# One load queue, halved K and V loads and a shared wq/wo buffer in a decode attention and FFN kernel

## Chip, cores, metric

The kernel runs on one core of one Trainium2 chip. The metric is device time in microseconds (us), median over executions. The span of a profile is about 2 us shorter than the time of the same execution. GB/s are bytes that the core's 16 DMA engines moved, over time. In the profiles PE is the matrix engine (PEld its loads of weights), DVE the vector engine, ACT the scalar engine and SP the engine that here only issues loads; SBUF and PSUM are the core's own memories.

## The reference

```python
# x: 4 x 1 x 512; 32 query heads, 8 K/V heads, head size 128; the last 4096 of 16384 cached positions
xn = layernorm(x)
q  = xn @ wq                                   # wq 512 x 4096
o  = softmax(q k^T / sqrt(128)) v              # per batch and head, window of 4096
A  = o @ wo                                    # wo 4096 x 512
B  = (silu(xn @ w_gate) * (xn @ w_up)) @ w_down  # F = 1792
out = x + A + B
```

There is one query position, so nearly everything is reading: 32 groups (4 batches by 8 K/V heads) of 1 MiB of K and 1 MiB of V each, 67.1 MB, and 13.9 MB of weights.

## The kernel before

Weights come first. The K buffers are allocated after the buffer of wq is released, and lie where it lay. K tiles are loaded from the SP queue, V tiles from the ACT queue, each tile in one transfer with 8 KiB a partition. For each group PE transposes K (stage_T), multiplies it by q (stage_QK), ACT takes the exp, and PE multiplies by V (stage_PV). After each fourth group four heads of the output projection run.

```python
wq_pool = tc.alloc_tile_pool(name="wq_pool", bufs=1)
wq_sb = wq_pool.tile([P, KT, HD], bf16, name="wq_sb")
nc.sync.dma_start(out=wq_sb[:, :, :], in_=A_wq.rearrange("(k p) n -> p k n", p=P))
# ... layer norm, FFN (PSUM pool of 2 buffers), query projection ...
wq_pool.release()
k_pool = ctx.enter_context(tc.tile_pool(name="k_pool", bufs=5))
# ...
def stage_load(b, hk):
    k_nat = k_pool.tile([P, NCH, Dh], bf16, tag="knat")
    v_t = v_pool.tile([P, NCH, Dh], bf16, tag="v")
    nc.sync.dma_start(out=k_nat[:, :, :],
        in_=A_k_cache[b, hk, W0:W0 + W, :].rearrange("(p c) d -> p c d", c=NCH))
    nc.scalar.dma_start(out=v_t[:, :, :],
        in_=A_v_cache[b, hk, W0:W0 + W, :].rearrange("(p c) d -> p c d", c=NCH))
# ...
for gi in range(NG):
    if gi_load < NG:
        load_q.append(stage_load(*groups[gi_load]))   # two groups ahead
        # ...
    if pv_q:   stage_PV(pv_q.popleft())
    if qk_q:   pv_q.append(stage_QK(qk_q.popleft()))
    if load_q: qk_q.append(stage_T(load_q.popleft()))
```

The framework that builds the program orders the instructions of each engine by priority and readiness, so the order on an engine isn't always the order of the source.

The softmax here doesn't subtract the row's maximum and nothing guards it: scores larger than these inputs give would overflow.

## Time and profile before

| | before |
|---|---|
| time, median | 219.15 us (6 runs, 216.78 to 220.46) |
| profiled span | 216.2 us, granted clock 0.871 |
| bytes moved | 81.47 MB |
| DMA engines busy | nearly all of 2 to 203 us |
| PE busy | 72% of the span |

A DMA share of 1.00 in a window means that all 16 engines had work; the GB/s beside it tell how fast that work went. Both are needed below: the share can stay at 1 while the rate changes. The windows below count a packet's bytes where it starts. A transfer has *landed* when its semaphore is set, which in these traces comes some 0.4 us after its last packet has ended; ends of the stream are compared by that. Here are the page's rows of DMA issues (bytes each, then the median time from issue to landing) before.

```profile
v_t<-in_A_v_cache_dram ACTq DMA_DIRECT2D x32, 1024.0 KB, 13.2
k_nat<-in_A_k_cache_dram SPq DMA_DIRECT2D x32, 1024.0 KB, 12.5
```

The last V load alone is issued at 190.5 us, and the same view of the issues between 189 and 200 us gives its landing:

```profile
v_t<-in_A_v_cache_dram ACTq DMA_DIRECT2D x1, 1024.0 KB, 13.6
```

So it lands at 204.1 us (204.05 before rounding), and 12.1 us of the span follow. The prediction below takes 203.2 us and 13.0 us, from the window in which the last packets start; the load is still ending in the first 0.9 us of that tail.

### The profile page before, as it was taken

The page shows a single profiled execution, that of the slowest core. Times are in us where ns is not written, and L with a number is a line of the kernel's source. Part 1 is how long each engine was busy: PE and PEld are TensorE (multiplying, and loading weights), DVE is VectorE, ACT ScalarE, POOL GpSimd, SP SyncE. Part 2 cuts the span into 40 slices and gives each one's busy share as a digit, 9 for nine tenths or more (in the row PEclk, how much of TensorE's full clock was granted, in tenths as well). Part 3 has the DMA queues.
Part 4 walks back from the last instruction along what each step waited for, and adds up shares of the span by engine and source line. Part 5 has one row for each costly group of instructions (what it writes and reads, how often), then busy time and mean ns, then how long its engine had stood idle before and what let it go on. Part 6 is the DMA issues. An engine that isn't in the chain of part 4 may idle for free.

```text
span 216.2 us, 7353 instructions
## 1 busy us (share of the span) xinstructions
PE 156.2 (72%) x3394; PEld 135.4 (63%) x3394; DVE 112.1 (52%) x300; ACT 14.7 (7%) x39; POOL 0.7 (0%) x6
## 2 busy tenths in 40 slices
PE   0000368830698799987969997899799969969983
PEld 0000254320697697985968797689769947966980
DVE  4000353130376565865747684458657754854771
ACT  2000502000001000000100000000001000000010
POOL 1000000000000000000000000000000000000000
PEclk9999999965589959999997998579969997995895
DMA  6999999999999999999999999999999999999300
GB/s 216 418 417 398 356 368 406 406 372 389 415 426 415 411 418 415 400 424 415 414 417 417 414 415 418 412 418 417 412 420 418 414 420 415 412 421 381 127 3 1
DMA packets 16765, 81.47 MB, mean 377 GB/s; under 512 B 1112, under 2 KB 7008, under 8 KB 8032
## 3 DMA queue, kind: packets, MB, share of 16 engines
q1 hardware_dynamic: 9784, 43.78, 50.7%
q10 hardware_dynamic: 6952, 37.23, 42.5%
q8 instruction: 26, 0.43, 0.8%
q14 instruction: 3, 0.02, 0.0%
HBM read 81.01 MB, written 0.00 MB: 375 GB/s over the span
## 4 chain that ended last, share of the span: by engine, by line
PE 67%; issue 16%; DVE 9%; DMA 5%; ACTq 1%; ACT 1%
PE tp L208 31%; PE oT_ps L232 12%; PE st_ps L217 11%; PE out_acc L182 6%; DMA k_nat<-in_A_k_cache_dram 5%; PE out_acc L145 3%; PE q_ps L155 2%; PE a_ps L126 2%; DVE qT_all L162 1%; DVE aT L130 1%; ACT L86 1%; PE den_ps L248 0%; ACTq L195 0%; DVE kt_4253 L209 0%; DVE kt_3657 L209 0%
## 5 line engine op out<-in xcount | busy, mean ns | idle before, releaser
L208 PE MATMUL tp<-ident,k_nat 128*128 128x128 bf16 x1024 | 88.5, 236 | 17.6 <-DMA k_nat<-in_A_k_cache_dram 9.9
L208 PEld LDWEIGHTS <-k_nat 128*128 128x128 bf16 x1024 | 67.3, 105 | 23.4 <-issue 23.2
L232 PE MATMUL oT_ps<-p_sb,v_t 128*128 128x4 bf16 x1024 | 33.6, 165 | 3.0 <-issue 2.6
L232 PEld LDWEIGHTS <-v_t 128*128 128x128 bf16 x1024 | 32.2, 98 | 5.0 <-issue 4.8
L225 ACT ACTIVATE p_sb<-st_ps 128x128 bf16<-128x128 f32 x32 | 8.9, 277 | 167.3 <-PE st_ps L217 158.9
L111 PE MATMUL tp<-ident,xn_bf 4*128 4x4 bf16 x4 | 0.4, 165 | 24.5 <-DVE xn_bf L103 24.3
L111 PEld LDWEIGHTS <-xn_bf 4*128 4x128 bf16 x4 | 0.3, 102 | 24.5 <-DVE xn_bf L103 24.3
L182 PE MATMUL out_acc<-wo_sb,oT_all 128*4 128x512 bf16 x32 | 13.0, 552 | 0.5 <-DVE oT_all L251 0.5
L101 DVE RECIPROCAL rstd<-std 4x1 f32<-4x1 f32 x1 | 0.2, 151 | 18.3 <-ACT std L99 18.3
L162 DVE CAST qT_all<-q_ps 128x4 bf16<-128x4 f32 x32 | 4.6, 174 | 9.4 <-PE q_ps L155 9.1
L250 DVE RECIPROCAL rec<-den_ps 128x4 f32<-128x4 f32 x32 | 5.6, 176 | 6.5 <-PE den_ps L248 6.1
L209 DVE COPY kt_553<-tp 128x1024 bf16<-128x1024 bf16 x4 | 2.8, 691 | 11.3 <-PE tp L208 11.3
L241 DVE TENSOR_REDUCE dsum<-p_sb 128x4 bf16<-128x128 bf16 x32 | 8.2, 276 | 0.5 <-ACT p_sb L225 0.5
L155 PE MATMUL q_ps<-xnT,wq_sb 128*128 128x4 bf16 x128 | 5.7, 165 | 2.7 <-DVE qT_all L162 2.4
L155 PEld LDWEIGHTS <-wq_sb 128*128 128x128 bf16 x128 | 4.7, 101 | 4.3 <-issue 4.3
L248 PE MATMUL den_ps<-dsum,ones 128*128 128x4 bf16 x32 | 5.4, 169 | 1.8 <-issue 1.8
L182 PEld LDWEIGHTS <-oT_all 128*4 128x4 bf16 x32 | 2.6, 99 | 5.7 <-issue 4.3
L145 PE MATMUL out_acc<-wd_sb,hT 128*4 128x512 bf16 x14 | 5.8, 604 | 0.0
L251 DVE TENSOR_TENSOR oT_all<-oT_ps,rec 128x4 bf16<-128x4 f32 x32 | 5.2, 163 | 0.6
L126 PEld LDWEIGHTS <-wg_sb 128*128 128x128 bf16 x56 | 3.7, 105 | 3.0 <-issue 2.9
L209 DVE COPY kt_3537<-tp 128x1024 bf16<-128x1024 bf16 x4 | 2.7, 688 | 4.6 <-PE tp L208 4.6
L126 PE MATMUL a_ps<-xnT,wg_sb 128*128 128x4 bf16 x56 | 3.5, 166 | 2.1 <-DVE xnT L112 0.3
(125 smaller groups left out, 182.7 us busy)
## 6 DMA issues: line engine op xcount, KB each, us to landing
v_t<-in_A_v_cache_dram ACTq DMA_DIRECT2D x32, 1024.0 KB, 13.2
k_nat<-in_A_k_cache_dram SPq DMA_DIRECT2D x32, 1024.0 KB, 12.5
wq_sb<-in_A_wq_dram SPq DMA_DIRECT2D x1, 4096.0 KB, 15.8
wo_sb<-in_A_wo_dram SPq DMA_DIRECT2D x1, 4096.0 KB, 51.7
wg_sb<-in_B_w_gate_dram SPq DMA_DIRECT2D x1, 1792.0 KB, 22.2
wu_sb<-in_B_w_up_dram ACTq DMA_DIRECT2D x1, 1792.0 KB, 17.8
wd_sb<-in_B_w_down_dram ACTq DMA_DIRECT2D x1, 1792.0 KB, 30.0
x_sb<-in_A_x_dram ACTq DMA_DIRECT2D x1, 4.0 KB
```

The source lines that it names most:

```text
L126: nc.tensor.matmul(a_ps[:, :], wg_sb[:, kt, ft * P:(ft + 1) * P], xnT[:, kt, :], start=(kt == 0), stop=(kt == KT - 1),)
L145: nc.tensor.matmul(out_acc[:, :], hT[:, ft, :], wd_sb[:, ft, :], start=(not acc_started[0]), stop=False,)
L155: nc.tensor.matmul(q_ps[:, :], wq_sb[:, kt, h * Dh:(h + 1) * Dh], xnT[:, kt, :], start=(kt == 0), stop=(kt == KT - 1),)
L162: nc.vector.tensor_copy(out=qT_all[:, :, h], in_=q_ps[:, :])
L182: nc.tensor.matmul(out_acc[:, :], oT_all[:, h, :], wo_sb[:, h, :], start=(not acc_started[0]), stop=is_last,)
L208: nc.tensor.transpose(tp[:, j, :], k_nat[:, c, :], ident[:, :])
L209: nc.vector.tensor_copy(out=kt2[:, tb * TCH:(tb + 1) * TCH, :], in_=tp[:, :, :])
L217: nc.tensor.matmul(st_ps[:, c * rep:(c + 1) * rep], kt2[:, c, :], q_g, start=True, stop=True,)
L225: nc.scalar.activation(p_sb[:, :], st_ps[:, :], Act.Exp, scale=inv_sqrt_dh)
L232: nc.tensor.matmul(oT_ps[:, :], v_t[:, c, :], p_sb[:, c * rep:(c + 1) * rep], start=(c == 0), stop=(c == NCH - 1),)
L241: nc.vector.tensor_reduce(dsum[:, :], p_sb[:, :].rearrange("n (c h) -> n h c", h=rep), axis=AXX, op=ADD,)
L250: nc.vector.reciprocal(rec[:, :], den_ps[:, :])
```

## The change

Its intent is to keep the stream of loads full and to shorten what is left when it ends. wo takes the buffer of wq, so K buffers exist from the start; all large loads go through the SP queue in one planned order; K and V tiles come in two halves each; K is requested 6 groups ahead and V 4; the FFN comes after the query projection, with one PSUM buffer instead of two.

```diff
-    wq_pool = tc.alloc_tile_pool(name="wq_pool", bufs=1)
-    wq_sb = wq_pool.tile([P, KT, HD], bf16, name="wq_sb")
+    wshared = wpool.tile([P, KT, HD], bf16, name="wshared")
+    wq_sb = wshared
+    wo_sb = wshared[:, :, :].rearrange("p k n -> p (k n)").rearrange("p (h d) -> p h d", d=D)
 ...
+    def stage_load_k(b, hk):
+        k_nat = k_pool.tile([P, NCH, Dh], bf16, tag="knat")
+        src = A_k_cache[b, hk, W0:W0 + W, :].rearrange("(p c) d -> p c d", c=NCH)
+        nc.sync.dma_start(out=k_nat[:, :HALF, :], in_=src[:, :HALF, :])
+        if NCH - HALF > 0:
+            nc.sync.dma_start(out=k_nat[:, HALF:, :], in_=src[:, HALF:, :])
+        return k_nat
 ...  (stage_load_v is the same for V, also on nc.sync)
-    with tc.tile_pool(name="ps_ffn", bufs=2, space=bass.MemoryType.PSUM) as ps_ffn:
+        with tc.tile_pool(name="ps_ffn", bufs=1, space=bass.MemoryType.PSUM) as ps_ffn:
 ...
-    nc.scalar.mul(mean[:, :], mean[:, :], 1.0 / D)
+    nc.vector.tensor_scalar_mul(mean[:, :], mean[:, :], 1.0 / D)
 ...  (loads of 6 K tiles, then 4 V tiles; two groups transposed; projection)
+    nc.sync.dma_start(out=wo_sb[:, :, :], in_=A_wo.rearrange("(h p) d -> p h d", p=P))
+    do_ffn()
 ...
+    for gi in range(PRE_T, NG):
+        issue_more_loads(1, 1)
```

More of the change, by code (lines that the diff above doesn't have):

```diff
@@ L50 @@
     assert NCH * rep <= 512 and rep <= P and NCH >= 1
+    assert KT * HD == Hq * D
     TCH = min(8, NCH)
@@ L63 @@
     nc.vector.memset(ones[:, :], 1.0)
-    x_sb = small.tile([B, D], bf16, name="x_sb")
-    nc.scalar.dma_start(out=x_sb[:, :], in_=A_x.rearrange("b s d -> (b s) d"))
-    wq_pool = tc.alloc_tile_pool(name="wq_pool", bufs=1)
-    wq_sb = wq_pool.tile([P, KT, HD], bf16, name="wq_sb")
-    nc.sync.dma_start(out=wq_sb[:, :, :], in_=A_wq.rearrange("(k p) n -> p k n", p=P))
+    wshared = wpool.tile([P, KT, HD], bf16, name="wshared")
+    wq_sb = wshared
+    wo_sb = wshared[:, :, :].rearrange("p k n -> p (k n)").rearrange("p (h d) -> p h d", d=D)
+    wq_view = A_wq.rearrange("(k p) n -> p k n", p=P)
+    half = max(1, KT // 2)
+    nc.sync.dma_start(out=wq_sb[:, :half, :], in_=wq_view[:, :half, :])
     wg_sb = wpool.tile([P, KT, F], bf16, name="wg_sb")
@@ L74 @@
     wd_sb = wpool.tile([P, FT, D], bf16, name="wd_sb")
-    wo_sb = wpool.tile([P, Hq, D], bf16, name="wo_sb")
-    nc.scalar.dma_start(out=wu_sb[:, :, :], in_=B_w_up.rearrange("(k p) f -> p k f", p=P))
-    nc.sync.dma_start(out=wg_sb[:, :, :], in_=B_w_gate.rearrange("(k p) f -> p k f", p=P))
-    nc.scalar.dma_start(out=wd_sb[:, :, :], in_=B_w_down.rearrange("(t p) d -> p t d", p=P))
+    x_sb = small.tile([B, D], bf16, name="x_sb")
+    nc.scalar.dma_start(out=x_sb[:, :], in_=A_x.rearrange("b s d -> (b s) d"))
@@ L80 @@
+    if KT - half > 0:
+        nc.sync.dma_start(out=wq_sb[:, half:, :], in_=wq_view[:, half:, :])
     out_acc = ps_out_pool.tile([B, D], f32, name="out_acc")
-    x_f32 = small.tile([B, D], f32, name="x_f32")
-    nc.vector.tensor_copy(out=x_f32[:, :], in_=x_sb[:, :])
-    mean = small.tile([B, 1], f32, name="mean")
-    nc.vector.reduce_sum(mean[:, :], x_f32[:, :], axis=AXX)
-    nc.scalar.mul(mean[:, :], mean[:, :], 1.0 / D)
-    xc = small.tile([B, D], f32, name="xc")
-    nc.vector.tensor_scalar(
-        out=xc[:, :], in0=x_f32[:, :], scalar1=mean[:, :], scalar2=None, op0=SUB
-    )
@@ L91 @@
-    junk = small.tile([B, D], f32, name="junk")
-    var = small.tile([B, 1], f32, name="var")
-    nc.vector.tensor_tensor_reduce(
-        out=junk[:, :], in0=xc[:, :], in1=xc[:, :], scale=1.0 / D, scalar=0.0,
-        op0=MULT, op1=ADD, accum_out=var[:, :],
-    )
-    nc.vector.tensor_scalar_add(var[:, :], var[:, :], 1e-5)
-    std = small.tile([B, 1], f32, name="std")
-    nc.scalar.activation(std[:, :], var[:, :], Act.Sqrt)
-    rstd = small.tile([B, 1], f32, name="rstd")
-    nc.vector.reciprocal(rstd[:, :], std[:, :])
@@ L102 @@
-    xn_bf = small.tile([B, D], bf16, name="xn_bf")
-    nc.vector.tensor_scalar(
-        out=xn_bf[:, :], in0=xc[:, :], scalar1=rstd[:, :], scalar2=None, op0=MULT
-    )
-    xnT = small.tile([P, KT, B], bf16, name="xnT")
-    with tc.tile_pool(name="ps_t", bufs=2, space=bass.MemoryType.PSUM) as ps_t:
-        for kt in range(KT):
-            tp = ps_t.tile([P, B], bf16, tag="tpx")
-            nc.tensor.transpose(tp[:, :], xn_bf[:B, kt * P:(kt + 1) * P], ident[:B, :B])
-            nc.vector.tensor_copy(out=xnT[:, kt, :], in_=tp[:, :])
@@ L114 @@
-    qT_all = small.tile([P, B, Hq], bf16, name="qT_all")
-    oT_all = small.tile([P, Hq, B], bf16, name="oT_all")
-    acc_started = [False]
-    heads_remaining = [Hq]
-    aT = small.tile([P, FT, B], f32, name="aT")
-    uT = small.tile([P, FT, B], f32, name="uT")
-    with tc.tile_pool(name="ps_ffn", bufs=2, space=bass.MemoryType.PSUM) as ps_ffn:
-        for ft in range(FT):
-            a_ps = ps_ffn.tile([P, B], f32, tag="ffn")
-            for kt in range(KT):
-                nc.tensor.matmul(
-                    a_ps[:, :], wg_sb[:, kt, ft * P:(ft + 1) * P], xnT[:, kt, :],
-                    start=(kt == 0), stop=(kt == KT - 1),
-                )
-            nc.vector.tensor_copy(out=aT[:, ft, :], in_=a_ps[:, :])
-            u_ps = ps_ffn.tile([P, B], f32, tag="ffn")
-            for kt in range(KT):
-                nc.tensor.matmul(
-                    u_ps[:, :], wu_sb[:, kt, ft * P:(ft + 1) * P], xnT[:, kt, :],
-                    start=(kt == 0), stop=(kt == KT - 1),
-                )
-            nc.vector.tensor_copy(out=uT[:, ft, :], in_=u_ps[:, :])
@@ L138 @@
-    sig = small.tile([P, FT, B], f32, name="sig")
-    nc.scalar.activation(sig[:, :, :], aT[:, :, :], Act.Sigmoid)
-    g = small.tile([P, FT, B], f32, name="g")
-    nc.vector.tensor_tensor(out=g[:, :, :], in0=aT[:, :, :], in1=sig[:, :, :], op=MULT)
-    hT = small.tile([P, FT, B], bf16, name="hT")
-    nc.vector.tensor_tensor(out=hT[:, :, :], in0=g[:, :, :], in1=uT[:, :, :], op=MULT)
-    for ft in range(FT):
-        nc.tensor.matmul(
-            out_acc[:, :], hT[:, ft, :], wd_sb[:, ft, :],
-            start=(not acc_started[0]), stop=False,
-        )
-        acc_started[0] = True
@@ L151 @@
-    with tc.tile_pool(name="ps_proj", bufs=2, space=bass.MemoryType.PSUM) as ps_proj:
-        for h in range(Hq):
-            q_ps = ps_proj.tile([P, B], f32, tag="proj")
-            for kt in range(KT):
-                nc.tensor.matmul(
-                    q_ps[:, :],
-                    wq_sb[:, kt, h * Dh:(h + 1) * Dh],
-                    xnT[:, kt, :],
-                    start=(kt == 0),
-                    stop=(kt == KT - 1),
-                )
-            nc.vector.tensor_copy(out=qT_all[:, :, h], in_=q_ps[:, :])
@@ L163 @@
-    wq_pool.release()
-    k_pool = ctx.enter_context(tc.tile_pool(name="k_pool", bufs=5))
-    kt2_pool = ctx.enter_context(tc.tile_pool(name="kt2_pool", bufs=4))
+    k_pool = ctx.enter_context(tc.tile_pool(name="k_pool", bufs=6))
+    kt2_pool = ctx.enter_context(tc.tile_pool(name="kt2_pool", bufs=3))
     v_pool = ctx.enter_context(tc.tile_pool(name="v_pool", bufs=5))
@@ L169 @@
     o_pool = ctx.enter_context(tc.tile_pool(name="o_pool", bufs=3))
-    ps_tp = ctx.enter_context(tc.tile_pool(name="ps_tp", bufs=2, space=bass.MemoryType.PSUM))
-    ps_s = ctx.enter_context(tc.tile_pool(name="ps_s", bufs=2, space=bass.MemoryType.PSUM))
-    ps_o = ctx.enter_context(tc.tile_pool(name="ps_o", bufs=2, space=bass.MemoryType.PSUM))
     groups = [(b, hk) for hk in range(Hkv) for b in range(B)]
     NG = len(groups)
-    WO_AT = min(NG - 1, 2)
+    LOOK = min(6, NG)
+    FFN_AT = min(NG, 8)
+    acc_started = [False]
+    ffn_done = [False]
+    pending_heads: list[int] = []
+    heads_remaining = [Hq]
     def issue_wo_matmuls(heads):
@@ L186, in issue_wo_matmuls, with stage_load_v @@
             acc_started[0] = True
-    def stage_load(b, hk):
+    HALF = max(1, NCH // 2)
+    def stage_load_k(b, hk):
         k_nat = k_pool.tile([P, NCH, Dh], bf16, tag="knat")
-        v_t = v_pool.tile([P, NCH, Dh], bf16, tag="v")
-        nc.sync.dma_start(
-            out=k_nat[:, :, :],
-            in_=A_k_cache[b, hk, W0:W0 + W, :].rearrange("(p c) d -> p c d", c=NCH),
-        )
-        nc.scalar.dma_start(
-            out=v_t[:, :, :],
-            in_=A_v_cache[b, hk, W0:W0 + W, :].rearrange("(p c) d -> p c d", c=NCH),
-        )
-        return (b, hk, k_nat, v_t)
+        src = A_k_cache[b, hk, W0:W0 + W, :].rearrange("(p c) d -> p c d", c=NCH)
[3 more added lines that the diff above has]
+        return k_nat
+    def stage_load_v(b, hk):
+        v_t = v_pool.tile([P, NCH, Dh], bf16, tag="v")
+        src = A_v_cache[b, hk, W0:W0 + W, :].rearrange("(p c) d -> p c d", c=NCH)
+        nc.sync.dma_start(out=v_t[:, :HALF, :], in_=src[:, :HALF, :])
+        if NCH - HALF > 0:
+            nc.sync.dma_start(out=v_t[:, HALF:, :], in_=src[:, HALF:, :])
+        return v_t
     def stage_T(st):
@@ L257, in stage_PV, with do_ffn @@
         if pb == B - 1:
-            issue_wo_matmuls(list(range(phk * rep, (phk + 1) * rep)))
-    LOOK = 2
+            heads = list(range(phk * rep, (phk + 1) * rep))
+            if ffn_done[0]:
+                issue_wo_matmuls(heads)
+            else:
+                pending_heads.extend(heads)
+    def do_ffn():
+        ffn_done[0] = True
+        aT = small.tile([P, FT, B], f32, name="aT")
+        uT = small.tile([P, FT, B], f32, name="uT")
+        with tc.tile_pool(name="ps_ffn", bufs=1, space=bass.MemoryType.PSUM) as ps_ffn:
+            for ft in range(FT):
+                a_ps = ps_ffn.tile([P, B], f32, tag="ffn")
+                for kt in range(KT):
+                    nc.tensor.matmul(
+                        a_ps[:, :], wg_sb[:, kt, ft * P:(ft + 1) * P], xnT[:, kt, :],
+                        start=(kt == 0), stop=(kt == KT - 1),
+                    )
+                nc.vector.tensor_copy(out=aT[:, ft, :], in_=a_ps[:, :])
+                u_ps = ps_ffn.tile([P, B], f32, tag="ffn")
+                for kt in range(KT):
+                    nc.tensor.matmul(
+                        u_ps[:, :], wu_sb[:, kt, ft * P:(ft + 1) * P], xnT[:, kt, :],
+                        start=(kt == 0), stop=(kt == KT - 1),
+                    )
+                nc.vector.tensor_copy(out=uT[:, ft, :], in_=u_ps[:, :])
+        sig = small.tile([P, FT, B], f32, name="sig")
+        nc.scalar.activation(sig[:, :, :], aT[:, :, :], Act.Sigmoid)
+        g = small.tile([P, FT, B], f32, name="g")
+        nc.vector.tensor_tensor(out=g[:, :, :], in0=aT[:, :, :], in1=sig[:, :, :], op=MULT)
+        hT = small.tile([P, FT, B], bf16, name="hT")
+        nc.vector.tensor_tensor(out=hT[:, :, :], in0=g[:, :, :], in1=uT[:, :, :], op=MULT)
+        for ft in range(FT):
+            is_last_acc = (ft == FT - 1) and heads_remaining[0] == 0 and not pending_heads
+            nc.tensor.matmul(
+                out_acc[:, :], hT[:, ft, :], wd_sb[:, ft, :],
+                start=(not acc_started[0]), stop=is_last_acc,
+            )
+            acc_started[0] = True
+        if pending_heads:
+            issue_wo_matmuls(list(pending_heads))
+            pending_heads.clear()
@@ new lines @@
+    nc.sync.dma_start(out=wg_sb[:, :, :], in_=B_w_gate.rearrange("(k p) f -> p k f", p=P))
+    nc.sync.dma_start(out=wu_sb[:, :, :], in_=B_w_up.rearrange("(k p) f -> p k f", p=P))
+    nc.sync.dma_start(out=wd_sb[:, :, :], in_=B_w_down.rearrange("(t p) d -> p t d", p=P))
+    k_tiles = {}
+    v_tiles = {}
+    for gi in range(LOOK):
+        k_tiles[gi] = stage_load_k(*groups[gi])
+    x_f32 = small.tile([B, D], f32, name="x_f32")
+    nc.vector.tensor_copy(out=x_f32[:, :], in_=x_sb[:, :])
+    mean = small.tile([B, 1], f32, name="mean")
@@ new lines @@
+    nc.vector.reduce_sum(mean[:, :], x_f32[:, :], axis=AXX)
+    nc.vector.tensor_scalar_mul(mean[:, :], mean[:, :], 1.0 / D)
+    xc = small.tile([B, D], f32, name="xc")
+    nc.vector.tensor_scalar(
+        out=xc[:, :], in0=x_f32[:, :], scalar1=mean[:, :], scalar2=None, op0=SUB
+    )
+    junk = small.tile([B, D], f32, name="junk")
+    var = small.tile([B, 1], f32, name="var")
+    nc.vector.tensor_tensor_reduce(
+        out=junk[:, :], in0=xc[:, :], in1=xc[:, :], scale=1.0 / D, scalar=0.0,
+        op0=MULT, op1=ADD, accum_out=var[:, :],
+    )
@@ new lines @@
+    nc.vector.tensor_scalar_add(var[:, :], var[:, :], 1e-5)
+    std = small.tile([B, 1], f32, name="std")
+    nc.scalar.activation(std[:, :], var[:, :], Act.Sqrt)
+    rstd = small.tile([B, 1], f32, name="rstd")
+    nc.vector.reciprocal(rstd[:, :], std[:, :])
+    V_LOOK = min(4, NG)
+    for gi in range(V_LOOK):
+        v_tiles[gi] = stage_load_v(*groups[gi])
+    xn_bf = small.tile([B, D], bf16, name="xn_bf")
+    nc.vector.tensor_scalar(
+        out=xn_bf[:, :], in0=xc[:, :], scalar1=rstd[:, :], scalar2=None, op0=MULT
+    )
@@ new lines @@
+    xnT = small.tile([P, KT, B], bf16, name="xnT")
+    with tc.tile_pool(name="ps_t", bufs=2, space=bass.MemoryType.PSUM) as ps_t:
+        for kt in range(KT):
+            tp = ps_t.tile([P, B], bf16, tag="tpx")
+            nc.tensor.transpose(tp[:, :], xn_bf[:B, kt * P:(kt + 1) * P], ident[:B, :B])
+            nc.vector.tensor_copy(out=xnT[:, kt, :], in_=tp[:, :])
+    qT_all = small.tile([P, B, Hq], bf16, name="qT_all")
+    oT_all = small.tile([P, Hq, B], bf16, name="oT_all")
+    ps_tp = ctx.enter_context(tc.tile_pool(name="ps_tp", bufs=2, space=bass.MemoryType.PSUM))
@@ L263, with issue_more_loads @@
     pv_q = deque()
-    for gi in range(min(LOOK, NG)):
-        load_q.append(stage_load(*groups[gi]))
-    gi_load = min(LOOK, NG)
-    for gi in range(NG):
-        if gi_load < NG:
-            load_q.append(stage_load(*groups[gi_load]))
-            if gi_load == WO_AT:
-                nc.sync.dma_start(out=wo_sb[:, :, :], in_=A_wo.rearrange("(h p) d -> p h d", p=P))
-            gi_load += 1
+    k_issued = LOOK
+    v_issued = V_LOOK
+    pending_kv = {}
+    def issue_more_loads(k_count, v_count):
+        nonlocal k_issued, v_issued
+        for _ in range(k_count):
+            if k_issued < NG:
+                k_tiles[k_issued] = stage_load_k(*groups[k_issued])
+                b_, hk_ = groups[k_issued]
+                load_q.append((b_, hk_, k_tiles[k_issued], k_issued))
+                k_issued += 1
+        for _ in range(v_count):
+            if v_issued < NG:
+                v_tiles[v_issued] = stage_load_v(*groups[v_issued])
+                v_issued += 1
+    for gi in range(LOOK):
+        b, hk = groups[gi]
+        load_q.append((b, hk, k_tiles[gi], gi))
+    PRE_T = min(2, NG)
+    for gi in range(PRE_T):
+        issue_more_loads(1, 1)
+        st = load_q.popleft()
+        qk_q.append(stage_T((st[0], st[1], st[2], v_tiles[st[3]])))
+    with tc.tile_pool(name="ps_proj", bufs=2, space=bass.MemoryType.PSUM) as ps_proj:
+        for h in range(Hq):
+            q_ps = ps_proj.tile([P, B], f32, tag="proj")
+            for kt in range(KT):
+                nc.tensor.matmul(
+                    q_ps[:, :],
+                    wq_sb[:, kt, h * Dh:(h + 1) * Dh],
+                    xnT[:, kt, :],
+                    start=(kt == 0),
+                    stop=(kt == KT - 1),
+                )
+            nc.vector.tensor_copy(out=qT_all[:, :, h], in_=q_ps[:, :])
+    nc.sync.dma_start(out=wo_sb[:, :, :], in_=A_wo.rearrange("(h p) d -> p h d", p=P))
+    do_ffn()
+    ps_s = ctx.enter_context(tc.tile_pool(name="ps_s", bufs=2, space=bass.MemoryType.PSUM))
+    ps_o = ctx.enter_context(tc.tile_pool(name="ps_o", bufs=2, space=bass.MemoryType.PSUM))
+    for gi in range(PRE_T, NG):
+        issue_more_loads(1, 1)
         if pv_q:
@@ L278 @@
         if load_q:
-            qk_q.append(stage_T(load_q.popleft()))
-    if NG - 1 < WO_AT:
-        nc.sync.dma_start(out=wo_sb[:, :, :], in_=A_wo.rearrange("(h p) d -> p h d", p=P))
+            st = load_q.popleft()
+            qk_q.append(stage_T((st[0], st[1], st[2], v_tiles[st[3]])))
+    if not ffn_done[0]:
+        do_ffn()
     while load_q or qk_q or pv_q:
@@ L285 @@
         if load_q:
-            qk_q.append(stage_T(load_q.popleft()))
+            st = load_q.popleft()
+            qk_q.append(stage_T((st[0], st[1], st[2], v_tiles[st[3]])))
         if qk_q:
             pv_q.append(stage_QK(qk_q.popleft()))
+    if pending_heads:
+        issue_wo_matmuls(list(pending_heads))
+        pending_heads.clear()
     res_bf = small.tile([B, D], bf16, name="res_bf")
```

## The prediction

> **What bounds the kernel now.** I read the page first, in its forty slices.
>
> ```profile
> PE   0000368830698799987969997899799969969983
> DMA  6999999999999999999999999999999999999300
> GB/s 216 418 417 398 356 368 406 406 372 389 415 426 415 411 418 415 400 424 415 414 417 417 414 415 418 412 418 417 412 420 418 414 420 415 412 421 381 127 3 1
> PE 156.2 (72%) x3394; PEld 135.4 (63%) x3394; DVE 112.1 (52%) x300; ACT 14.7 (7%) x39; POOL 0.7 (0%) x6
> ```
>
> The DMA row is full from slice 1 to slice 36, and falls to 3, 0, 0 in the last three, where PE still works. So there are two stages: some 201 us in which 81.47 MB are streamed without a gap, and a tail in which the stream has ended and PE empties its pipeline. Next I read the end in short windows (PE, PEld, DVE, ACT, POOL, then clock, DMA share, GB/s).
>
> ```profile
> 198.00:200.00 2.00, 2.00 (x11) 0.84 (x10) 0.03 (x1) 0.00 (x0) 0.00 (x0) 0.50 0.74 299
> 202.00:203.00 1.00, 1.00 (x30) 1.00 (x27) 0.12 (x2) 0.28 (x1) 0.00 (x0) 1.00 0.53 221
> 203.00:204.00 1.00, 1.00 (x36) 1.00 (x34) 1.00 (x2) 0.00 (x0) 0.00 (x0) 1.00 0.11 33
> 204.00:206.00 2.00, 2.00 (x59) 2.00 (x57) 1.84 (x5) 0.00 (x0) 0.00 (x0) 1.00 0.00 0
> ```
>
> The last byte comes at about 203.2 us (33 GB/s in the 203 window, nothing after). The span is 216.2 us, so the tail is 13.0 us. The chain of waits says what the tail holds: transposes, scores and value products of the last groups until 210, then this.
>
> ```profile
> 210.02 0.94 PE oT_ps L232 x32
> 211.48 1.78 PE out_acc L182 x4
> 213.29 0.68 DVE res_bf L291
> ```
>
> The last group's value product starts at 210.02 and the kernel ends 6.2 us later. The 6.8 us from 203.2 to 210.0 are work for which all data had landed. The reason is in the waits of the issuing queue.
>
> ```profile
> SPq L191 <- PE tp L208: 67.4, 19, 6.9
> SPq L191 <- DMA wd_sb<-in_B_w_down_dram: 29.5, 1, 29.5
> SPq L191 <- DMA v_t<-in_A_v_cache_dram: 27.3, 8, 6.9
> SPq L191 <- PE q_ps L155: 14.3, 1, 14.3
> ```
>
> K loads wait for transposes to free one of 5 buffers, and the first K load waits for the query projection, because the K buffers lie where wq lay. The first K load is issued at 46.18 us and PE starts on it at 56.06. From there PE does 32 groups until the last transpose near 208.5: 4.76 us a group. Two K/V tiles are 2.10 MB, or 5.04 us at 416 GB/s. PE is thus a little quicker than the stream, but started late and is still behind when the stream ends.
>
> **What the Trainium skill says.** (1) "DMA: Bandwidth & Descriptors", section "Issuing engines are not separate DMA queues": transfers issued from different engines run on the same 16 DMA engines, and a second issuing engine only saves issue time. The trace agrees: two queues gave 415 to 416 GB/s between 65 and 195 us. So putting everything on one queue costs no bandwidth by itself. (2) The same page, section "Bandwidth", gives about 358 GB/s as the HBM limit of one core. The trace disagrees (416), and I use the trace. (3) The same page, the load-stream table in "SWDGE vs HWDGE vs iDMA", has 408.7 GB/s for 1 MiB loads with 4 KiB rows from SP; this case's 8 KiB rows show 416, and nothing before has 4 KiB rows. (4) "TensorE: Matmul & The Clock Gate", Part 1: the array falls to half clock after an idle window. The trace agrees: eight transposes take 0.88 us where the clock is 0.50 and 0.47 us where it is 1.00.
>
> **The change, part by part.**
>
> *Order of loads and the wq/wo buffer.* The bytes are the same. wq no longer shares space with K, so K loads need not wait for the projection; wo waits for it instead. K and V tiles are requested 6 and 4 groups ahead, and K stays two groups ahead of V. The last transfers are therefore V29, V30, V31, without a K between the last two. When V31 lands, transposes and scores of group 31 can be done. What remains is the chain above with half a value product (0.94/2): 6.2 - 0.5, plus my estimate of 0.5 us for the semaphore, is 6.2 us of tail for 13.0. **Gain 6.8 us.** This needs PE to keep up. It should: V30 and V31 take 5 us to stream, about one group's PE work, and PE starts on K some 25 us earlier than now.
>
> *Halved K and V loads.* Rows of 4 KiB replace rows of 8 KiB. What a row costs comes from these windows.
>
> ```profile
> 27.00:29.00 2.00, 1.42 (x33) 1.17 (x32) 1.07 (x9) 0.00 (x0) 0.00 (x0) 1.00 1.09 349
> 57.00:61.00 4.00, 4.00 (x57) 3.90 (x56) 2.76 (x4) 0.00 (x0) 0.00 (x0) 0.50 1.02 426
> 61.00:65.00 4.00, 3.94 (x107) 3.81 (x106) 3.19 (x7) 0.28 (x1) 0.00 (x0) 0.95 1.02 424
> 125.00:165.00 40.00, 35.59 (x788) 31.43 (x786) 24.59 (x57) 2.22 (x8) 0.00 (x0) 0.83 1.01 416
> ```
>
> At 27 to 29 us only wd and wo stream, both with 1 KiB rows: 1024 x 16 / 349 = 46.9 ns a row on one engine. At 57 to 64 us the V queue is empty (it issued at 32.16, then at 64.14), and K alone, 8 KiB rows, runs at 425: 308.4 ns. A line through both has 36.5 ps a byte and 9.6 ns a row, so a 4 KiB row takes 159 ns, or 412 GB/s (an estimate; the skill's 408.7 is near). Note that the single queue's 425 is above the 416 of two queues. The 67.1 MB of K and V then take 162.9 us instead of 161.3. **Cost 1.6 us.** Issue is no cost: 128 issues at 0.33 us are 42 us of an otherwise idle queue.
>
> *ACT freed.* ACT now sits 18.61 us in the issue of its first V load (3.38 to 22.0), and the square root of the layer norm waits behind it for 18.1 us. With V on the other queue the normalised x is ready near 7.5 us, and the projection can run when wq has landed (2.3 us start + 4.19 MB at 421, about 12.5 us) until about 21: sixteen pairs of heads at 0.51 us. This is off the path that sets the end, but it is what lets PE start on K early. The mean's scaling moving from ACT to DVE saves a hop of under 1 us, hidden.
>
> *FFN with one PSUM buffer.* Now two groups of four matmuls share a 0.50 us round; with one buffer each needs its own (0.26 + 0.17 + hand-overs 0.06), so 28 x 0.49 = 13.7 us for 7.0. It lies between about 22 and 40 us, where the stream is still bringing K0 to K5, and transposes can fill its gaps. **Cost on the path: 0.** Score buffers in PSUM come after it, so scores begin near 40 us, and the first value product near 46, when V0 has landed.
>
> *Starting.* Up to V4 and K7 no load needs a value product: 9.7 MB of weights and 13.6 MB of K and V keep the stream busy to about 60 us, to 72 with wo. V5, which waits for the first value product, asks at 46. So no gap, if wo is not stuck behind V5. For that and for small bubbles I add **1.0 us**.
>
> Sum: -6.8 + 1.6 + 1.0 = -4.2 us; span 216.2 to 212.0, and the median 219.15 to about **214.9 us**. As the row cost may be overstated (windows with 3.5 KiB rows beside 8 KiB ones reached 424), I shade it by 0.4 to 214.5.
>
> **Rivals.** (a) *The stream stays the bound and rows of 4 KiB cost more.* At 402 GB/s they would cost 5.6 us instead of 1.6: 218.5 us. For it: the long mean of 416 is already below 425, and the loss may add up. Against: single-queue K ran at 425. (b) *A new wait in the one issuing queue.* A V load waiting for its buffer now also holds back K behind it, and the K issues already wait for transfers of other tiles (27.3 and 29.5 us above), so there is a limit on the transfers in flight; half-size transfers halve the bytes under it. If the first value product came after 72 us, every us later is a us lost: 218 to 223 us. Against: in steady state four K/V pairs are allowed ahead of PE. (c) *PE becomes the bound.* If transposes of two groups go ahead of the projection and the slow FFN follows unfilled, PE's loop starts near 60 us as now, the tail stays, and the time is 218 to 220. Against: weights land before K, and now PE already fills gaps with work from other stages. (d) *Better than thought:* single-queue speed of 420 and no bubbles: 211.
>
> **Range and chances.** The centre is 214.5; (d) sets the low end at 210.5, (a) and mild (b) or (c) the high end at 218.5. The 2% line is 214.8, so the centre lies on it: faster 0.53, same 0.39, slower (over 223.5, only a bad b) 0.08.
>
> **What would show it.** Right: DMA full to about 204 or 205 us; K/V windows at 410 to 415 GB/s; a tail of 6 to 7 us from last byte to end, with the last value product waiting for its V transfer; PE with idle time put down to K or V loads. Wrong: K/V windows near 400 (a), a dip in the DMA row around 50 to 75 us (b), or a tail still over 10 us with transposes in it (c).

## The result

| | before | after |
|---|---|---|
| time, median | 219.35 us (40 runs) | 216.49 us (20 runs) |
| range of the runs | 216.78 to 224.11 | 216.36 to 216.78 |
| profiled span | 216.2 us | 214.6 us |
| ratio, 95% interval | | 0.9908 (0.9885 to 0.9932) |

The ratio is the mean time of one kernel's fast runs over that of the other's fast runs of the same rounds, so it isn't quite the ratio of the medians: the runs of the kernel before that lie over 1.5% above its fastest one count as slow and are left out of it. The change is 0.9% faster, less than the 2% from which the prediction speaks of faster; 2.1% had been predicted. The spread of the runs shrank from 7.3 to 0.4 us.

The page's slices after the change:

```profile
PE   0136459999779369789999789879989988989974
DMA  6999999999999999999999999999999999999930
GB/s 224 428 408 403 352 405 407 411 405 408 408 391 348 351 406 406 405 412 405 407 408 404 406 407 405 413 405 405 407 410 407 407 403 408 405 409 402 359 128 1
```

PE starts work in slice 1 (counted from 0) and not in slice 4, and the DMA row is full for one slice longer. The number to look at is the plain one: from slice 14 to slice 35, where only K and V stream, the rate is 403 to 413, 407 on average; before it was 400 to 424, 416 on average. Here is the end in windows of 1 us (PE, PEld, DVE, ACT, POOL, then clock, DMA share, GB/s), to set against the 203 window of before.

```profile
202.00:203.00 1.00, 0.66 (x16) 0.64 (x16) 0.90 (x2) 0.00 (x0) 0.00 (x0) 0.92 0.79 303
206.00:207.00 1.00, 0.80 (x27) 0.67 (x24) 0.29 (x3) 0.00 (x0) 0.00 (x0) 0.50 0.48 180
208.00:209.00 1.00, 0.41 (x16) 0.32 (x12) 0.18 (x1) 0.00 (x0) 0.00 (x0) 0.50 0.03 12
```

The last V lands at 209.0 us, where before it landed at 204.1. The chain that ended last (start, length, what):

```profile
197.31 11.70 DMA v_t<-in_A_v_cache_dram
209.05 0.60 PE oT_ps L157 x16
209.90 1.88 PE out_acc L102 x4
211.80 0.68 DVE res_bf L344
```

That is the tail as the prediction drew it: the last half of V lands at 209.01, half a value product follows, then the last four heads, the residual and the store. It is 5.6 us long, for 12.1 before. So **the tail gave 6.5 us and the stream took back 5.0**: 216.16 - 6.51 + 4.96 = 214.61. The waits of the issuing queue after the change (total us, times, longest):

```profile
SPq L121 <- DMA v_t<-in_A_v_cache_dram: 24.7, 25, 2.5
SPq L115 <- DMA k_nat<-in_A_k_cache_dram: 23.9, 24, 2.5
SPq L121 <- PE tp L133: 3.0, 6, 2.0
```

Before, this queue waited 67.4 us for transposes to free buffers. Now it waits for earlier transfers, and hardly for PE: the stream sets the pace alone. That also fits the narrow spread of the times, since the part that varied with PE is off the path; this reading isn't tested further.

### The profile page after: what moved, and what is told of

Same layout as the page of the kernel before. It is cut to its first block, busy times and chain, and to the rows that moved or that the text cites. A ratio compares the mean times of both kernels' runs of the same rounds, so it can differ in the third digit from the quotient of the medians.

```text
span 214.6 us, 7409 instructions
## 1 busy us (share of the span) xinstructions
PE 168.5 (79%) x3394; PEld 145.6 (68%) x3394; DVE 115.4 (54%) x301; ACT 13.2 (6%) x37; POOL 0.7 (0%) x6
## 4 chain that ended last, share of the span: by engine, by line
DMA 73%; PE 17%; DVE 6%; issue 2%; SPq 1%
DMA v_t<-in_A_v_cache_dram 64%; DMA wu_sb<-in_B_w_up_dram 9%; PE tp L133 7%; PE st_ps L142 3%; PE oT_ps L157 3%; PE out_acc L217 1%; PE u_ps L204 1%; DVE kt_223 L134 1%; PE a_ps L197 1%; PE out_acc L102 1%; DVE aT L201 1%; DVE uT L208 1%; DVE kt_1316 L134 1%; DVE kt_702 L134 1%; DVE kt_824 L134 0%
## 5 line engine op out<-in xcount | busy, mean ns | idle before, releaser
L133 PEld LDWEIGHTS <-k_nat 128*128 128x128 bf16 x1024 | 74.7, 114 | 9.4 <-issue 6.1
L157 PE MATMUL oT_ps<-p_sb,v_t 128*128 128x4 bf16 x1024 | 35.5, 165 | 4.6 <-issue 2.9
L157 PEld LDWEIGHTS <-v_t 128*128 128x128 bf16 x1024 | 31.3, 99 | 5.3 <-issue 3.1
L102 PE MATMUL out_acc<-wshared,oT_all 128*4 128x512 bf16 x32 | 12.4, 531 | 7.1 <-DMA wshared<-in_A_wo_dram 4.8
L166 DVE TENSOR_REDUCE dsum<-p_sb 128x4 bf16<-128x128 bf16 x32 | 9.0, 285 | 10.8 <-ACT p_sb L150 10.6
L307 PE MATMUL q_ps<-xnT,wshared 128*128 128x4 bf16 x128 | 5.9, 166 | 8.9 <-DMA wshared<-in_A_wq_dram 6.4
L307 PEld LDWEIGHTS <-wshared 128*128 128x128 bf16 x128 | 4.8, 105 | 10.0 <-DMA wshared<-in_A_wq_dram 6.6
L134 DVE COPY kt_1438<-tp 128x1024 bf16<-128x1024 bf16 x4 | 2.8, 691 | 7.4 <-PE tp L133 7.4
L204 PEld LDWEIGHTS <-wu_sb 128*128 128x128 bf16 x56 | 3.6, 105 | 4.1 <-issue 3.4
L204 PE MATMUL u_ps<-xnT,wu_sb 128*128 128x4 bf16 x56 | 3.5, 167 | 3.2 <-DVE aT L201 2.5
L134 DVE COPY kt_824<-tp 128x1024 bf16<-128x1024 bf16 x4 | 2.8, 689 | 4.2 <-PE tp L133 3.1
L134 DVE COPY kt_4122<-tp 128x1024 bf16<-128x1024 bf16 x4 | 2.8, 692 | 3.7 <-PE tp L133 3.6
## 6 DMA issues: line engine op xcount, KB each, us to landing
k_nat<-in_A_k_cache_dram SPq DMA_DIRECT2D x64, 512.0 KB, 10.2
v_t<-in_A_v_cache_dram SPq DMA_DIRECT2D x64, 512.0 KB, 10.2
```

What stands on the lines that cost most here:

```text
L102: nc.tensor.matmul(out_acc[:, :], oT_all[:, h, :], wo_sb[:, h, :], start=(not acc_started[0]), stop=is_last,)
L133: nc.tensor.transpose(tp[:, j, :], k_nat[:, c, :], ident[:, :])
L134: nc.vector.tensor_copy(out=kt2[:, tb * TCH:(tb + 1) * TCH, :], in_=tp[:, :, :])
L157: nc.tensor.matmul(oT_ps[:, :], v_t[:, c, :], p_sb[:, c * rep:(c + 1) * rep], start=(c == 0), stop=(c == NCH - 1),)
L166: nc.vector.tensor_reduce(dsum[:, :], p_sb[:, :].rearrange("n (c h) -> n h c", h=rep), axis=AXX, op=ADD,)
L204: nc.tensor.matmul(u_ps[:, :], wu_sb[:, kt, ft * P:(ft + 1) * P], xnT[:, kt, :], start=(kt == 0), stop=(kt == KT - 1),)
```

## The experiments

Two questions. Why is the stream 5.0 us longer? And was the tail shortened for the reason given? My theory for the first: rows of 4 KiB (bytes that one partition gets in one piece) are dearer than I had reckoned. Rivals: the single queue, or the smaller and more numerous transfers. All results were correct. Times of the kernel before in these rounds had medians of 219.29 to 219.65 us.

### e1: whole K and V loads, one queue

```diff
-        nc.sync.dma_start(out=k_nat[:, :HALF, :], in_=src[:, :HALF, :])
-        nc.sync.dma_start(out=k_nat[:, HALF:, :], in_=src[:, HALF:, :])
+        nc.sync.dma_start(out=k_nat[:, :, :], in_=src[:, :, :])   # and V alike
```

> The changed kernel with each K and V tile loaded whole again (8 KiB rows, 1 MiB transfers), still on one queue. Row theory (4 KiB rows cost the stream 2.3%): K/V windows return from 407 to at least 416 GB/s, the end of the stream comes 3.6 us earlier or more, the time is 211 to 213.5 us, ratio to before 0.965 to 0.975. If the prediction's claim holds that one queue is faster than two, 425 GB/s and 209.5 us (0.957). Rival (one queue is what costs): windows stay at 407 and the time at 216.5 or a little more (0.99 to 0.995).

Measured: 213.19 us, ratio 0.9741 (0.9678 to 0.9803). First a window of the stage where only K and V stream, after the change and then in e1; the rest is e1's chain.

```profile
125.00:165.00 40.00, 35.57 (x758) 31.33 (x759) 24.38 (x56) 2.22 (x8) 0.00 (x0) 0.83 1.03 407
```

```profile
125.00:165.00 40.00, 36.43 (x766) 32.86 (x764) 25.46 (x53) 1.94 (x7) 0.00 (x0) 0.79 1.01 417
```

```profile
186.48 18.60 DMA v_t<-in_A_v_cache_dram
205.12 1.01 PE oT_ps L153 x32
```

The last V now lands at 205.08 us, 3.9 us earlier than in the change. The rate is back to 416 and 417 GB/s, and the four runs (213.04 to 213.32 us) all lie below those of the change. One queue costs the rate nothing: this is the 416 of the two queues before. But neither does it gain: 425 didn't come, and the prediction's claim that a single queue is faster fell here.

### g4: whole loads, short rows

e1 changed row length and transfer size together. This run changes row length alone: the tile in SBUF has one unused chunk after each half, so a transfer of 1 MiB still writes pieces of 4 KiB.

```diff
-        k_nat = k_pool.tile([P, NCH, Dh], bf16, tag="knat")
+        k_nat = k_pool.tile([P, 2, HALF + 1, Dh], bf16, tag="knat")
-        nc.sync.dma_start(out=k_nat[:, :, :], in_=src[:, :, :])
+        nc.sync.dma_start(out=k_nat[:, :, :HALF, :], in_=src[:, :, :, :])  # src "(p h c) d -> p h c d"
```

> Whole K and V loads as in e1 (1 MiB, one transfer per tile), but the tile in SBUF has a gap of 256 bytes between its halves, so that the rows written are 4 KiB again. Row theory: 407 GB/s in K/V windows and 216.5 to 217.5 us (the stream of the change, the tail of e1), ratio 0.99. Rival (the size or number of transfers is what cost, not the rows): 416 GB/s and 213.2 us, ratio 0.974.

Measured: 217.04 us, ratio 0.9934 (0.9910 to 0.9957).

```profile
125.00:165.00 40.00, 36.19 (x757) 32.35 (x755) 24.56 (x54) 2.22 (x8) 0.00 (x0) 0.79 1.02 406
```

```profile
189.68 19.66 DMA v_t<-in_A_v_cache_dram
209.38 1.01 PE oT_ps L153 x32
```

With as many transfers as e1, and of the same size, but 24974 DMA packets for e1's 16782, the rate is that of the change and the last V lands at 209.34. Row length alone costs 4.3 us of stream and 3.85 us of time (217.04 - 213.19, medians of different rounds). The rival of transfer size is out.

### f6: quarters

```diff
-        nc.sync.dma_start(out=k_nat[:, :HALF, :], in_=src[:, :HALF, :])
-        nc.sync.dma_start(out=k_nat[:, HALF:, :], in_=src[:, HALF:, :])
+        for h4 in range(4):
+            cs = slice(h4 * NCH // 4, (h4 + 1) * NCH // 4)
+            nc.sync.dma_start(out=k_nat[:, cs, :], in_=src[:, cs, :])
```

> The changed kernel with K and V in quarters: 2 KiB rows, 256 KiB transfers. Row theory, with 51 ns for a 1 KiB row and 163 ns for a 4 KiB row: 2 KiB take about 88 ns, 370 to 380 GB/s, the stream ends 11 to 16 us later: 227 to 233 us, ratio 1.04 to 1.06. Rival (only the count of transfers in flight costs, rows cost nothing): 407 GB/s wherever the stream has no gap, and gaps in it.

Measured: 234.49 us, ratio 1.0658 (1.0554 to 1.0763), just above the range. The profiled run counts as slow, so only its rates are read.

```profile
40.00:60.00 20.00, 18.67 (x449) 16.31 (x449) 12.04 (x31) 2.95 (x7) 0.00 (x0) 0.96 1.04 373
125.00:165.00 40.00, 34.98 (x666) 28.95 (x664) 21.79 (x47) 1.95 (x7) 0.00 (x0) 0.78 1.02 363
```

2 KiB rows go at 373 GB/s in the early stage, as the row theory said, and slower later, which it didn't say; no fast run of f6 has a profile. Transfers of a quarter tile land after 5.6 us, halves after 10.2 and whole tiles after 20; the number in flight is thus about constant (2.1 MB over 5.6 us, 4.2 over 10.2, 8.4 over 20 are eight transfers in each), and with quarters few bytes are in flight. Whether that explains the 363 was not tried.

### e3 and e4: two queues with 4 KiB rows

e3 is the change with V on the ACT queue; e4 is the kernel before with only the loads halved.

```diff
# e3: stage_load_v of the change, both halves
-        nc.sync.dma_start(out=v_t[:, :HALF, :], in_=src[:, :HALF, :])
+        nc.scalar.dma_start(out=v_t[:, :HALF, :], in_=src[:, :HALF, :])
# e4: stage_load of the kernel before, K and V alike
-        nc.sync.dma_start(out=k_nat[:, :, :], in_=...)
+        nc.sync.dma_start(out=k_nat[:, :HALF, :], in_=k_src[:, :HALF, :])
+        nc.sync.dma_start(out=k_nat[:, HALF:, :], in_=k_src[:, HALF:, :])
```

> The changed kernel, halves of 4 KiB rows kept, V loads moved to the ACT queue. Row theory: 407 GB/s stays, time 216 to 217.5 (0.99). Rival (one queue is what costs): 412 to 416 GB/s and about 213 us (0.973).

> The kernel before with only the K and V loads halved (4 KiB rows, two queues). Row theory: K/V windows at 407 instead of 416; the stream ends 3.5 us later; the tail may shrink by part of it, since PE was behind the stream; time 219 to 223 us, ratio 1.00 to 1.016. Rival (one queue is what costs): 416, ratio 1.00 or under.

Measured: e3 225.72 us, ratio 1.0222 (1.0096 to 1.0347), its profile slow; e4 227.51 us, ratio 1.0396 (1.0323 to 1.0470). Both are slower than either theory said. Windows of e3, then of e4:

```profile
85.00:125.00 40.00, 31.90 (x640) 27.49 (x637) 20.04 (x47) 1.83 (x7) 0.00 (x0) 0.71 0.98 352
125.00:165.00 40.00, 34.55 (x707) 30.75 (x706) 23.13 (x52) 1.83 (x7) 0.00 (x0) 0.77 1.02 405
```

```profile
48.00:54.00 6.00, 0.00 (x0) 0.00 (x0) 0.00 (x0) 0.00 (x0) 0.00 (x0) 0.50 0.91 308
125.00:165.00 40.00, 36.28 (x767) 32.40 (x765) 24.70 (x54) 2.22 (x8) 0.00 (x0) 0.79 1.03 406
```

Where the stream runs evenly it goes at 405 to 407, so the number of queues doesn't matter for the rate, with 4 KiB rows as with 8. The rest of the loss is in stretches with a low rate. In e4 the K loads wait up to 23.0 us for V transfers, as the queue's waits show. In the window from 48 to 54 PE stands still, as it does in the kernel before, but the rate is 308 GB/s, where it is 385 before. Both runs say that halved loads can cost more than the rows do; that the waits for earlier transfers are the reason is argued here, not tested.

### e2: halves by partition

Each tile in two transfers of 64 partitions by 8 KiB.

```diff
-        nc.sync.dma_start(out=k_nat[:, :HALF, :], in_=src[:, :HALF, :])
-        nc.sync.dma_start(out=k_nat[:, HALF:, :], in_=src[:, HALF:, :])
+        nc.sync.dma_start(out=k_nat[:P // 2, :, :], in_=src[:P // 2, :, :])
+        nc.sync.dma_start(out=k_nat[P // 2:, :, :], in_=src[P // 2:, :, :])
```

> The changed kernel with each tile in two transfers of 64 partitions by 8 KiB rows: same count and size of transfers as the change (512 KiB), rows as before. Row theory: as with whole loads, 416 GB/s or more, ratio 0.965 to 0.98. Rival (the smaller, more numerous transfers or fewer bytes in flight cost): 407 GB/s, ratio 0.99. If 64 partitions use only half of the engines at a time, it may be slower than both, and then the run says nothing on rows.

Measured: 327.38 us (310.89 to 339.26), the profiled run slow, 246 GB/s at a DMA share of 1.02 between 125 and 165 us. The run says nothing on rows; it had been named as possible. The Trainium skill has it in "SBUF — State Buffer", section "Door 1: The DMA port swizzle": 64 partitions in one half reach only half of the ports. The run agrees: the engines are fully busy at little over half of the rate (246 for 407).

### f5: two PSUM buffers in the FFN

```diff
-        with tc.tile_pool(name="ps_ffn", bufs=1, space=bass.MemoryType.PSUM) as ps_ffn:
+        with tc.tile_pool(name="ps_ffn", bufs=2, space=bass.MemoryType.PSUM) as ps_ffn:
```

> The changed kernel with two PSUM buffers in the FFN instead of one. Prediction's step (the slower FFN is off the path): FFN some 5 us quicker in the trace, time 216.5 us within 0.5, ratio 0.99. Rival (the late start of scores behind the FFN costs): 213 to 215 us.

Measured: 216.74 us, ratio 0.9883 (0.9823 to 0.9943): the time of the change. The last matmul of gate and up starts at 29.1 us, where in the change it starts at 41.2, a gain of 12 us and not the 5 expected. So the slower FFN is off the path.

### g2, g3 and f3: what shortened the tail

g2 is the kernel before with the shared buffer alone, so that K loads can go out early. g3 is e1 with V on the ACT queue. f3 is the change with the K lead taken away.

```diff
# g2, in the kernel before; the K, V and work pools move up to the weights
-    wq_pool = tc.alloc_tile_pool(name="wq_pool", bufs=1)
-    wq_sb = wq_pool.tile([P, KT, HD], bf16, name="wq_sb")
+    wshared = wpool.tile([P, KT, HD], bf16, name="wshared")
+    wq_sb = wshared
+    wo_sb = wshared[:, :, :].rearrange("p k n -> p (k n)").rearrange("p (h d) -> p h d", d=D)
# g3, in e1
-        nc.sync.dma_start(out=v_t[:, :, :], in_=src[:, :, :])
+        nc.scalar.dma_start(out=v_t[:, :, :], in_=src[:, :, :])
# f3, in the change
-    LOOK = min(6, NG)
+    LOOK = min(4, NG)
```

> The kernel before with one part of the change alone: wo shares the buffer of wq, so K buffers are free from the start and K loads go out early; K and V stay whole, paired, on two queues. If the earlier start of PE is what let PE keep up with the stream: stream at 416 to 203 or 204 us, last transposes 3 to 4 us after the last byte, tail 9 us, 214 to 216 us, ratio 0.98. If the lead of K over V is what matters: PE is as far behind at the end as before, tail 13 us, 219 us, ratio 1.00.

> e1 with V on the ACT queue: whole loads, 8 KiB rows, two queues. Gap-free windows at 416 as in e1. If one queue is what makes the run-out at half rate longer (6.2 us in the change and in e1, 4.4 us before): run-out 4.4 us, and about 211.5 us if the stream stays without gaps. As in e3 the V loads then wait in the queue of the exp instructions, and gaps as there (10 us) may hide it: then 220 us or more and nothing on the run-out.

> The changed kernel with K requested 4 groups ahead like V, so that the last K lands only 2.6 us before the last V. Tail theory of the prediction (K two groups ahead shortens the tail): the stream ends as in the change, but transposes (3.3 us at the low clock), scores and exp of group 31 end 2 to 3 us after V31 has landed: 218.5 to 220 us, ratio 1.00. Rival (it is the earlier start of PE that shortens the tail, the order of K and V does nothing): 216.5 us, ratio 0.991.

| | time, us | ratio (95%) | last K lands | last V lands | tail after both |
|---|---|---|---|---|---|
| before | 219.35 | | 201.6 | 204.1 | 12.1 |
| g2 | 217.77 | 0.9965 (0.993 to 1.000) | 204.6 | 204.0 | 12.7 |
| g3 | 217.32 | 0.9958 (0.9924 to 0.9992) | 201.6 | 203.8 | 11.4 |
| f3 | 251.13 | 1.1437 (1.1362 to 1.1513) | 211.8 | 215.4 | 32.2 |
| e1 | 213.19 | 0.9741 (0.9678 to 0.9803) | 196.1 | 205.1 | 6.3 |

In g2 the K loads are issued from 1.8 us on, yet PE begins its transposes only at 50.5 us: V loads still hold up ACT and with it the layer norm (PE waited 28.5 us for it), and FFN and projection come first. PE later waits for K loads nine times, 9.2 us in all, so it does keep up with the stream, and still the tail is as long as before. So free buffers alone shorten nothing. In g3 the rate is 417 and the tail 11.4. There K is asked for two groups ahead of V as in e1, but it didn't come ahead: the last K, issued at 181.4 us, took 20.2 us to land (the view of the issues from 181 to 200 us), and landed only 2.2 us before the last V.

```profile
k_nat<-in_A_k_cache_dram SPq DMA_DIRECT2D x1, 1024.0 KB, 20.2
```

With an uneven end of its stream (238 GB/s from 196 to 197), g3 says nothing clear about the run-out it was also meant for.

f3 missed both expectations. This is its window, with the clock before the last two columns, and two lines of its chain:

```profile
125.00:165.00 40.00, 34.67 (x584) 30.59 (x583) 20.33 (x42) 1.66 (x6) 0.00 (x0) 0.54 1.02 403
```

```profile
230.00 1.73 PE tp L133 x16
236.30 1.73 PE tp L133 x16
```

One group takes PE 6.30 us between these two lines (in the tail) and 5.9 to 8.5 us in the window, more than the 5.15 us that the stream takes for it (2.10 MB at 407 GB/s), so PE becomes the bound. The timeline shows what differs: with K no longer ahead, the program was ordered so that PE transposes, scores and multiplies by V the same group in turn, waiting inside each group for DVE (43 waits, 14.3 us in all) and for the exp (26 waits, 9.5 us), and the granted clock is 0.54 in this window, for 0.83 in the change. In the change PE works on another group's value product in between; it waits 8.1 us for DVE's copies, and no wait for the exp is listed. How much each of the two costs was not tried. So f3 changed PE's order as well as the tail, and can't tell the share of the K lead in the tail. What the runs show together: the shared buffer alone (g2) is not enough; the tail is 11 us or more where the last K lands within 2.5 us of the last V (before, g2, g3), and about 6 us where it lands 8 to 9 us earlier (e1, g4, f2, g1). No run changed that lead alone, so that it is the cause is supported, not shown, and whether K could lead on two queues was not tested.

### f2 and g1: a version that beats both

f2 is e1 with weights laid out so that each partition reads one run: row k of wq, wg and wu goes to partition k // 4, the FFN's hidden units likewise to partition f // 14, with strided slices on PE in return. g1 also puts the denominator's matmul ahead of the value product and halves the very last V tile.

```diff
-    wq_view = A_wq.rearrange("(k p) n -> p k n", p=P)
+    wq_view = A_wq.rearrange("(p k) n -> p k n", k=KT)          # wg, wu alike
-    ... B_w_down.rearrange("(t p) d -> p t d", p=P))
+    ... B_w_down.rearrange("(p t) d -> p t d", t=FT))
-            nc.tensor.transpose(tp[:, :], xn_bf[:B, kt * P:(kt + 1) * P], ident[:B, :B])
+            nc.tensor.transpose(tp[:, :], xn_v[:B, :, kt], ident[:B, :B])
-                        a_ps[:, :], wg_sb[:, kt, ft * P:(ft + 1) * P], xnT[:, kt, :],
+                        a_ps[:, :], wg_v[:, kt, :, ft], xnT[:, kt, :],
```

> Whole K and V loads on one queue (as e1), and wq, wg, wu and wd laid out so that each partition reads one contiguous run (16, 14, 14 and 14 KiB instead of rows of 8, 3.5, 3.5 and 1 KiB). Row theory: wd's 1.84 MB go at 416 instead of 349 GB/s, 0.85 us less, wg and wu some 0.3 us less: 212 us against e1's 213.2, ratio 0.967. Rival (the weights' part of the stream is not on the path that sets the end, or strided weight loads on PE cost it back): 213.2 or more.

> Wide weights and whole loads (as f2), with the denominator's matmul put ahead of the value product and the very last V tile in halves. Tail of f2: value product 1.01 and denominator and reciprocal 0.28 us after the last V; with this half a product and no denominator: 0.8 us less, 210.7 us, ratio 0.961. Rival (the last V's halves land together): 211.2 us.

Measured: f2 211.54 us, ratio 0.9646 (0.9598 to 0.9693); g1 211.06 us, ratio 0.9678 (0.9619 to 0.9737). The ratios were taken in different rounds; g1's four runs lie between 210.96 and 211.22 and f2's between 211.45 and 211.74, so g1 is the faster by about 0.5 us, less than the 0.8 expected and near the 211.2 of its rival; but that rival's reason fails, since the last V's halves landed apart, at 202.2 and 203.5 us. The two parts of g1 weren't separated. In f2 the slice of the page in which wd streams (slice 4) went from 352 GB/s in e1 to 409, which bears out the row theory on another tile. The chain of g1:

```profile
185.22 18.25 DMA v_t<-in_A_v_cache_dram
203.51 0.60 PE oT_ps L169 x16
204.35 1.88 PE out_acc L102 x4
```

The last V lands at 203.46, and 5.7 us of tail follow: the tail of the change on a stream of long rows. g1 is 3.2% faster than the kernel before by the fast runs, and 2.5% faster than the change by medians of different rounds.

## Why the prediction was right or wrong

| term | predicted, us | measured, us | from |
|---|---|---|---|
| tail | -6.8 | -6.5 | 12.1 to 5.6 in the two profiles |
| 4 KiB rows | +1.6 | +3.9 | last V at 209.0 after, at 205.1 in e1 |
| start and bubbles | +1.0 | +1.0 | last V at 205.1 in e1, at 204.1 before |
| sum | -4.2 | -1.6 | spans 216.2 and 214.6 |

- **What bounds the kernel** was right: the stream is gap-free in both, and the part that had to shrink was the tail.
- **The tail** was right in size and in its chain of instructions; the value product does wait for its V half (0.65 us at 209.05). By the prediction's own measure, the start of the last packets, it went to 6.2 us as forecast (they start at 208.4); only its words that in the 6.8 us before 210.0 "all data had landed" are 0.9 us too wide. PE started on K 24.6 us earlier (31.4 for 56.1 us). Of the two reasons, that and K ahead of V, the first alone is not enough: g2 shows a PE that keeps up with the stream and a tail of 12.7 us.
- **The row cost is the step that failed.** The prediction put a line through 1 KiB rows at 349 GB/s and 8 KiB rows at 425, a stretch of 8 us early in the main stage, and took the 416 of the long windows as the rate of two queues. It then set a row cost that started from 425 against a bill that started from 416, and so counted on a gain of the single queue inside it. e1 showed that there is none: one queue, 8 KiB rows, 416 to 417. With 416 as the base, the same line gives 315.1 ns for an 8 KiB row, 37.4 ps a byte and 8.6 ns a row, so 161.8 ns or 405 GB/s for 4 KiB, and 165.7 - 161.3 = 4.4 us. The runs show 407 and 3.9. What made the 425 between 57 and 65 us is open.
- **The shading by 0.4 us** went the wrong way for the same reason: windows near 424 early in the run were taken as the rate of the later stage.
- **Start and bubbles** had the right size, but for another reason: there was no gap (407 from 40 to 60 us), and the run-out took the time. When the last transfers are in flight, the rate falls to half and the share with it; that would fit some engines being done while others aren't, but the record has no times of single engines. From 198 us on, GB/s in windows of 1 us are 369, 229, 205, 229, 221, 33 before, and 311, 238, 197, 205, 188, 25, 16 in e1; from 202 us on they are 303, 225, 234, 209, 180, 25, 12 after. At 198 us e1 had less left to move than the kernel before (1.18 MB for 1.29), and yet its last V landed 1.0 us later. All the kernels with one queue that end on V have a longer run-out than the kernel before; the cause is open.
- **FFN at no cost on the path** was right (f5), and so were the estimates of the start: projection from 13.2 to 21.2 us (12.5 to 21 predicted), scores from 41.8 (40). The first value product came at 51.7 us and not 46, which cost nothing.
- **Rivals**: (a), dearer rows, is what happened, near the size named there (402 GB/s and 5.6 us, where 407 and 3.9 were measured). (b) and (c) did not happen in the change; (c) happened in f3. (d) did not happen: e1's single queue gave 416 to 417. The centre of the prediction left (a) out by choice of its base. By the prediction's own terms (a) comes to 214.9 - 1.6 + 5.6 = 218.9 us; its 218.5 keeps the shading of a cost that (a) replaces.

## What to carry to other kernels

When a stream is the bound, halving a load so that its first half can be used earlier also shortens the rows, and every byte of the stream pays for what only the last tile gains: here the halves took 0.7 us off the tail (6.3 in e1, 5.6 in the change) and put 3.9 us on the stream. Keep rows long, and split at most the last tile, as g1 does. Take the rate that a cost is set against from the stage that changes, not from a faster stretch elsewhere in the trace. And check what lands last when the stream ends, by landing times and not by the order in the source: the short tails here all came with the last K 8 to 9 us ahead of the last V.

## What the Trainium skill lacked or had wrong

- "DMA: Bandwidth & Descriptors", section "Specifications", gives 512 B as the smallest transfer for line rate. The runs show a slope far above it: 349 GB/s with 1 KiB rows, 373 with 2 KiB (early stage of f6, a slow profile), 407 with 4 KiB and 416 with 8 KiB, all with the DMA share at 1 or above. The table of load streams in the same page has 408.7 for 4 KiB rows, which agrees.
- The same page, "Bandwidth", says in its warning on three numbers that about 358 GB/s binds a transfer between HBM and SBUF; one core alone streamed at 416 here. The same section's own table (425 for 16 MB with the pair's other core idle) and "HBM Reference", section "Specifications (TRN2)" (a core alone measures about 425) are nearer. The prediction named only the 358.
- No page that I read has the run-out: for some 5 us at the end of a 200 us stream the rate is near half (180 to 240 GB/s) with a share near 0.5.
